# The run length and the pacing of the expert weights that are loaded during the attention

## The chip, the cores and the metric

The kernel runs on one core of a Trainium2 chip. Its engines are TensorE (PE in the profile, with its weight loads as PEld), VectorE (DVE), ScalarE (ACT), GpSimd (POOL) and SyncE (SP, which here only issues transfers). Sixteen DMA engines move the data between HBM and the on-chip memory. The metric is the device time of one execution in microseconds (us), as the median of several runs.

## The reference, cut to what matters

Three layers in a row: attention with a window and global tokens, a soft mixture of 8 experts, and a two-layer network with a squared ReLU. The change touches the weights of the second one, `w1` and `w2` (8 experts, 16 MB each).

```python
# 1. attention: 4 batches x 8 heads, 512 local + 32 global queries, head size 64
out_g = matmul(softmax(q_g @ k_all.T / 8), v_all)
out_l = softmax(window of 32 around each local query, and the 32 global keys) @ v
x = concat([out_g, out_l]) as (2176 tokens, 512)
# 2. soft mixture of experts
logits = x @ phi                                  # (2176, 32): 8 experts x 4 slots
d = softmax(logits, over tokens)
slot_input = (d.T @ x).reshape(8, 4, 512)
for e in range(8):
    h = maximum(slot_input[e] @ w1[e], 0.0)       # w1: (8, 512, 1024)
    slot_out[e] = h @ w2[e]                       # w2: (8, 1024, 512)
x = softmax(logits, over slots) @ slot_out
# 3. relu-squared network
return (maximum(x @ w_in, 0) ** 2) @ w_out        # w_in, w_out held as 64-bit floats
```

## The kernel before, in words

The program has three stages. The **attention** takes the first 156 us. It is cut into 32 steps, four for each of 8 groups (a batch and half of its heads). Each engine executes its instructions in the order in which the program writes them, and that order comes from a list: `at(when, fn)` puts a piece of work at a position `when`, counted in steps, and the list is sorted by `when`. A step `n` has its scores (`emit_S`: matmuls into `s`, line L397, then on VectorE the masked minimum, L404, and on ScalarE the exponentials, L408), its transposes (`emit_T`: `pT`, L416) and its products with the values (`emit_PV`: `X`, L428). The steps of the global queries (`glob_S`, `glob_T`, `glob_PV`: `sg`, `ggT`, `Xg`) and the running token softmax stand between them.

The **expert stage** (about 156 to 190 us) has one block of weights for each of 32 pieces of work: `hidden(q, kc)` uses a block of `w1` (L878, into `hp`), `outputs(q, m)` one of `w2` (L906, into `so`). A block is 1 MB: 128 partitions, two experts, 1024 words of 4 bytes for each. The trace has 8 records of PE for each block. The **last stage** (from 190 us) is the third layer, with matmuls into `ops` that fill PE.

The blocks are loaded ahead by SyncE, in the order of their use. They lie in a ring of 22 buffers: 13 with the tag `w`, which are free from the start, 5 with the tag `k`, in which the attention keeps q, k and v first (so a block can go there only when the attention has read them for the last time), and 4 with the tag `m`, freed at the attention's end. Later blocks take the place of used ones. So 18 blocks (13 + 5) are meant to be loaded while the attention runs.

- Blocks 0 to 12 are loaded by `ring_halves` in two halves, one for each expert of the pair, each half as two transfers of 256 KB. In each transfer a partition receives one run of 2 KB. The list `PACE` says at which positions a half is issued. Where it names an engine (`"dve"`), that engine first writes one element of the half; the transfer has to wait for that write (L172), so it can't start before VectorE has come to that place in its own work.
- Blocks 13 to 17, and later ones, are loaded by `more_weights` in one transfer of 1 MB, in runs of 4 KB (L157), once `RELEASE` at a position has raised the limit: three blocks at 25.85, one at 27.75, one at 29.15, two at 30.85. They have no pacing write. SyncE waits at each for the buffer to be free.

All transfers of SyncE share eight semaphores in turn, so each one waits until the one eight places before it has landed. SyncE's queue is in order: whatever stands behind a waiting transfer waits too. The loads of q, k and v go through SyncE and, for most of v, through GpSimd's queue; the last of them is issued before 120 us.

Of the kernel before, what the change touches and what calls it, by code (L numbers as in the profile page):

```python
# [9 lines left out]
F32 = mybir.dt.float32  # L10
# [40 lines left out]
POS = {'load0': -7.545, 'sort0': -5.099, 'sort1': -3.55, 'glob_S': 1.806, 'glob_T': 2.7, 'glob_PV': 3.655, 'w1': -2.548, 'w4': -0.34, 'w7': -0.339, 'w10': -1.245, 'w13': 1.7, 'v0': -1.648, 'v1': 0.25, 'x0': 1.756, 'x1': 2.555, 'x2': 3.8, 'x3': 4.158, 'L': 5.351, 'E': 5.8, 'sl': 6.752, 'qg': 1.158}  # L51
LASTPOS = {('glob_S', 6): 0.55, ('glob_T', 6): 1.75, ('glob_PV', 6): 3.35, ('glob_S', 7): -0.3, ('glob_T', 7): 0.35, ('glob_PV', 7): 1.7, ('v0', 7): 0.05, ('v1', 7): 2.05, ('w1', 1): -0.75, ('v0', 0): -0.75, ('sort0', 1): -5.95}
QGF = 0
RELEASE = ((25.85, 3), (27.75, 1), (29.15, 1), (30.85, 2))
EP = 'dve'
EQ = 'act'
EK = 'act'
# [5 lines left out]
PACE = [(2.9, 1, None), (3.9, 1, None)]  # L63
PACE += [(4 * k + d, 1, w) for k in range(1, 6) for d, w in ((0.9, None), (1.7, "dve"), (2.95, None), (3.9, None))]
PACE += [(24.9, 2, None), (25.45, 2, "dve")]
RECTS = 'A0-1 B0-2 C0-4 A2-6 B3-8 C5-10 A7-12 B9-15 A13-15 C11-15'
RING = 13
MORE = 5
# [8 lines left out]
def kernel(  # L77
# [7 lines left out]
    nc = tc.nc  # L85
    const = ctx.enter_context(tc.tile_pool(name="const", bufs=1))
    ring = ctx.enter_context(tc.tile_pool(name="ring", bufs=RING, side="right"))
# [20 lines left out]
    for kind, q in UNITS:  # L108
        es = slice(2 * q, 2 * q + 2)
        for m in range(4):  # L110
            src = (
                w1[es, m * 128:(m + 1) * 128, :].rearrange("e p f -> p e f") if kind == "w1" else
                w2[es, m * 256:(m + 1) * 256, :].rearrange("e (p t) d -> p e (t d)", t=2)
            )
# [3 lines left out]
        specs.insert(i, (("raw", raw_half), None))  # L118
    wt, raw = {}, {}
    w_in32, w_out32 = w_in.bitcast(I32), w_out.bitcast(I32)  # L120
    st = {"next": 0, "limit": RING}

    def slot(tag, shape, dt, nm):
        return ring.tile(shape, dt, tag=tag, name=nm, bufs={"w": RING, "k": MORE, "m": LAST}[tag])
# [36 lines left out]
    part = {}  # L161

    def ring_halves(n, paced):

        for _ in range(n):
            key, src = specs[st["next"]]
            c = part.get("c", 0)
            if c == 0:
                part["t"] = slot("w", list(src.shape), F32, f"ring{st['next']}")
            t = part["t"]  # L170
            if paced:
                (nc.vector if paced == "dve" else nc.gpsimd).memset(t[0:1, c, 0:1], 0.0)  # L172
            for x in (0, 512):
                nc.sync.dma_start(out=t[:, c, x:x + 512], in_=src[:, c, x:x + 512])
            part["c"] = 1 - c
            if c:
                wt[key] = t
                st["next"] += 1
# [527 lines left out]
    def at(when, fn, *args):  # L706
        order.append((when, len(order), fn, args))
# [44 lines left out]
    for when, n, paced in PACE:  # L752
        at(when, ring_halves, n, paced)
    for when, n in RELEASE:
        at(when, release, n)
# [317 lines left out]
    rects = []  # L1073
    for r in RECTS.split():
        a, e = map(int, r[1:].split("-"))
# [167 lines left out]
    for n in range(len(seq)):  # L1243
        credit = min(credit + RATE, 1.2)
        if pieces and n >= START and min(free) <= n:
            kind, f, a, fs = pieces[0]
            if n >= due[kind, f] or (credit >= 1 and not ntile[max(n - 1, -1)]):
                d = 2
# [4 lines left out]
                d = min(d, late)  # L1253
# [61 lines left out]
```

## Time and profile before

| | us |
|---|---|
| median of 3 runs (lowest to highest) | 421.16 (419.94 to 423.27) |
| the profiled execution | 421.35 |
| its span, from the first to the last instruction | 419.3 |
| PE busy | 387.4 (92%) |
| PEld busy | 284.2 (68%) |
| ACT busy | 291.6 (70%) |
| DVE busy | 290.8 (69%) |
| POOL busy | 68.4 (16%) |

Busy times are those of one execution. PE's records overlap a little and their ends are modelled, so 92% is no measure of how near PE is to its peak; where PE waited, and for what, is read from the chain of waits. The transfers moved 70.30 MB, at 168 GB/s over the span, but not evenly: most of it lies ahead of 200 us.

### The profile page before, as it was taken

To read this page: it belongs to the slowest core of one execution; us is meant where nothing else is said; L and a number is where in the kernel's file an instruction comes from. 1 tells how busy PE (TensorE), PEld (TensorE's weight loads), DVE (VectorE), ACT (ScalarE), POOL (GpSimd) and SP (SyncE) were. 2 spreads that over 40 slices of the span, in tenths; PEclk is the share of its full clock that TensorE was granted. 3 is DMA by queue.
4 is the path that set the end of the run, shared out by engine and by line. 5 is a ranking of instruction groups with operands and counts; after the bars stand their busy time and mean duration, and the time that the engine had idled before them with its cause. 6 is when DMAs were issued, how large, how long until landed. Compare 5 with 4: busy or idle time off the path is not lost.

```text
span 419.3 us, 11740 instructions
## 1 busy us (share of the span) xinstructions
PE 387.4 (92%) x4510; PEld 284.2 (68%) x4510; DVE 290.8 (69%) x903; ACT 291.6 (70%) x692; POOL 68.4 (16%) x169
## 2 busy tenths in 40 slices
PE   7978888977997889999899999999999999999995
PEld 6756656655773763336676878878787887888883
DVE  2878668868876541666999967878779776726623
ACT  3649787777895731137997988879688886876670
POOL 7336535535362010000000000000000000000000
PEclk9999999999999999999999999999999999999999
DMA  7668686898998999999431606033030000004403
GB/s 194 142 164 237 214 248 161 256 231 230 264 278 321 361 383 402 400 395 376 144 111 52 202 0 197 6 101 100 2 100 2 1 1 2 0 0 152 150 2 125
DMA packets 50199, 70.30 MB, mean 168 GB/s; under 512 B 16960, under 2 KB 33344, under 8 KB 50144
## 3 DMA queue, kind: packets, MB, share of 16 engines
q1 hardware_dynamic: 48512, 66.40, 48.4%
q0 software_dynamic: 1632, 3.15, 3.7%
q8 instruction: 36, 0.59, 0.6%
q14 instruction: 19, 0.16, 0.1%
HBM read 65.08 MB, written 4.46 MB: 166 GB/s over the span
## 4 chain that ended last, share of the span: by engine, by line
PE 69%; DMA 9%; ACT 8%; DVE 7%; issue 4%; SPq 2%; DVEq 0%; ACTq 0%
PE ops L1120 13%; PE ops L1121 13%; PE ops L1122 13%; DMA ring<-in_moe_w_dram 4%; PE hps L1085 4%; PE s L397 3%; DMA qk<-in_k_l_dram 3%; PE X L428 3%; PE hp L878 2%; PE pT L416 2%; ACT pbuf L408 2%; PE xTp L509 1%; DMA keys<-in_k_l_dram 1%; ACT x_g L499 1%; PE busy L662 1%
## 5 line engine op out<-in xcount | busy, mean ns | idle before, releaser
L1120 PE MATMUL ops<-hl,gh 128*128 128x512 f32 x266 | 105.8, 398 | 0.6 <-DVE oacc L1134 0.3
L1121 PE MATMUL ops<-hl,gh 128*128 128x512 f32 x266 | 105.7, 397 | 0.0
L1122 PE MATMUL ops<-hl,gl 128*128 128x512 f32 x266 | 104.9, 394 | 0.0
L1109 DVE TENSOR_TENSOR gl<-r,gh 128x384 fp32r<-128x384 f32 x96 | 49.8, 531 | 26.0 <-ACT r L1104 25.8
L1092 ACT ACTIVATE r<-hps 128x384 f32<-128x384 f32 x96 | 45.0, 469 | 22.9 <-PE hps L1085 21.7
L1120 PEld LDWEIGHTS ops<-hl,gh 128*128 128x128 f32 x266 | 49.9, 188 | 13.5 <-DVE oacc L1134 1.3
L1122 PEld LDWEIGHTS ops<-hl,gl 128*128 128x128 f32 x266 | 50.1, 188 | 12.2
L408 ACT ACTIVATE pbuf<-pbuf,nm 128x128 f32<-128x128 f32 x128 | 41.1, 393 | 24.8 <-DVE nm L404 24.5
L1121 PEld LDWEIGHTS ops<-hl,gh 128*128 128x128 f32 x266 | 50.0, 188 | 8.1 <-DVE hl L971 0.3
L1100 ACT ACTIVATE gh<-r 128x384 fp32r<-128x384 f32 x96 | 48.8, 508 | 3.0
L1104 ACT ACTIVATE r<-r 128x384 f32<-128x384 f32 x96 | 48.6, 507 | 3.0
L1085 PE MATMUL hps<-cT,wst 128*128 128x384 f32 x96 | 33.7, 353 | 1.2 <-ACT r L1092 1.2
L404 DVE CUSTOM_DVE_ANT_0 pbuf<-s,tbuf 128x128 f32<-128x128 f32 x128 | 29.6, 286 | 6.8 <-PE s L397 6.1
L1136 DVE SCALAR_TENSOR_TENSOR oacc<-ops,oacc 128x512 f32<-128x512 f32 x38 | 24.7, 686 | 4.1 <-PE ops L1122 4.0
L942 ACT ACTIVATE sgvm<-sgvm,ebias 128x512 int32<-128x512 int32 x32 | 22.8, 714 | 6.4 <-DVE sgvm L936 6.3
L1085 PEld LDWEIGHTS hps<-cT,wst 128*128 128x128 f32 x96 | 18.0, 188 | 8.4 <-issue 2.3
L416 PE MATMUL pT<-ident,pbuf 128*128 128x128 f32 x128 | 21.2, 289 | 2.7 <-ACT tbuf L186 2.7
L280 POOL DMA_DIRECT2D v<-in_v_l_dram x36 | 23.4, 659 | 0.0
L948 DVE SCALAR_TENSOR_TENSOR sgvm<-raw,sgvm 128x512 int32<-128x512 int32 x32 | 21.9, 685 | 1.0 <-ACT sgvm L942 1.0
L945 DVE SCALAR_TENSOR_TENSOR sgvm<-raw,sgvm 128x512 f32<-128x512 uint32 x32 | 21.9, 685 | 0.1
L416 PEld LDWEIGHTS pT<-ident,pbuf 128*128 128x128 f32 x128 | 13.9, 143 | 8.5 <-ACT tbuf L186 3.7
L971 DVE TENSOR_TENSOR hl<-sgvm,hl 128x512 fp32r<-128x512 f32 x16 | 11.0, 690 | 11.4 <-ACT hl L966 11.3
(202 smaller groups left out, 672.9 us busy)
## 6 DMA issues: line engine op xcount, KB each, us to landing
ring<-in_moe_w_dram SPq DMA_DIRECT2D x18, 1024.0 KB, 10.5
ring<-in_moe_w_dram SPq DMA_DIRECT2D x52, 256.0 KB, 5.3
raw<-in_moe_w_in_dram SPq DMA_DIRECT2D x16, 512.0 KB, 4.2
raw<-in_moe_w_out_dram SPq DMA_DIRECT2D x16, 512.0 KB, 5.0
out_dram<-oacc SPq DMA_DIRECT2D x16, 256.0 KB, 2.1
qk<-in_q_l_dram SPq DMA_DIRECT2D x15, 256.0 KB, 3.7
qk<-in_k_l_dram SPq DMA_DIRECT2D x15, 256.0 KB, 4.1
v<-in_v_l_dram POOLq DMA_DIRECT2D x30, 96.0 KB, 5.4
```

The source lines that it names most:

```text
L404: nc.vector.tensor_tensor_reduce(out=dst, in0=ps[h % 2][:, h // 2, :], in1=mask[:, uu, :], scale=1.0, scalar=FAR, op0=ALU.add, op1=ALU.min ...
L408: nc.scalar.activation(out=dst, in_=dst, func=AF.Exp, bias=nm[:, h:h + 1], scale=-1.0)
L416: nc.tensor.transpose(ps[:, 128 * h:128 * h + 128], pt[:, h, :], ident)
L1085: nc.tensor.matmul(ps, wst[:, f, :], cT[:, t0:t0 + n], start=True, stop=True)
L1092: nc.scalar.activation(out=r, in_=ps, func=AF.Relu)
L1100: nc.scalar.activation(out=gh, in_=r, func=AF.Square)
L1104: nc.scalar.activation(out=r, in_=r, func=AF.Square)
L1109: eng.tensor_tensor(out=gL, in0=sq, in1=gh.bitcast(F32), op=ALU.subtract)
L1120: nc.tensor.matmul(ob[tt], gh[:, s], hi, start=first, stop=False)
L1121: nc.tensor.matmul(ob[tt], gh[:, s], lo, start=False, stop=False)
L1122: nc.tensor.matmul(ob[tt], gL[:, s], hi, start=False, stop=last)
L1136: nc.vector.scalar_tensor_tensor(out=t, in0=ps, scalar=WS, in1=t, op0=ALU.mult, op1=ALU.add)
```

## The change

Blocks 0 to 12 are still loaded in two halves of two transfers each, but a half is now half of the columns of both experts and no longer the whole of one expert. Each transfer still moves 256 KB, now as two runs of 1 KB in each partition. Blocks 13 to 17 are loaded in the same way, four transfers of 256 KB, in place of one of 1 MB with 4 KB runs. Their halves stand at 25.87, 26.27, and so on to 28.67 (eight halves), and at 29.15 and 29.55, each behind a write of one element by VectorE. `RELEASE` keeps only the two blocks at 30.85. From block 18 on everything is loaded as before.

```diff
-RELEASE = ((25.85, 3), (27.75, 1), (29.15, 1), (30.85, 2))
+RELEASE = ((30.85, 2),)
...
 PACE += [(24.9, 2, None), (25.45, 2, "dve")]
+PACE += [(25.87 + 0.4 * x, 1, "dve") for x in range(8)]
+PACE += [(d, 1, "dve") for d in (29.15, 29.55)]
...
-    st = {"next": 0, "limit": RING}
+    st = {"next": 0, "limit": RING + MORE}
...
             if c == 0:
-                part["t"] = slot("w", list(src.shape), F32, f"ring{st['next']}")
+                tag = "w" if st["next"] < RING else "k"
+                part["t"] = slot(tag, list(src.shape), F32, f"ring{st['next']}")
             t = part["t"]
             if paced:
-                (nc.vector if paced == "dve" else nc.gpsimd).memset(t[0:1, c, 0:1], 0.0)
-            for x in (0, 512):
-                nc.sync.dma_start(out=t[:, c, x:x + 512], in_=src[:, c, x:x + 512])
+                nc.vector.memset(t[0:1, 0, 512 * c:512 * c + 1], 0.0)
+            for x in (512 * c, 512 * c + 256):
+                nc.sync.dma_start(out=t[:, :, x:x + 256], in_=src[:, :, x:x + 256])
             part["c"] = 1 - c
```

On SyncE, before, from the last transfer of block 12 (`ring12`; the number behind a ring is the block's) to the second of the last stage's buffers; the names in brackets are what a transfer waits for, DMAHW being the eight shared semaphores and DMASW those of GpSimd's queue:

```order
L174 DMA ring12_2823<-in_moe_w1_dram 128x512 [waits DMAHW0_49]
L157 DMA ring13_2871<-in_moe_w1_dram 128x2x1024 [waits DMAHW1_49,PE_49,Activation_49]
L157 DMA ring14_2873<-in_moe_w1_dram 128x2x1024 [waits DMAHW2_49,PE_49]
L157 DMA ring15_2875<-in_moe_w1_dram 128x2x1024 [waits DMAHW3_49,PE_49]
L157 DMA ring16_3048<-in_moe_w2_dram 128x2x1024 [waits DMASW3_49,DMASW2_49,DMASW4_49,DMASW1_49,DMASW5_49,DMASW0_49,DMAHW4_49,PE_49,Pool_49]
L157 DMA ring17_3144<-in_moe_w2_dram 128x2x1024 [waits DMAHW5_49,PE_49,Activation_49]
L157 DMA ring18_3257<-in_moe_w2_dram 128x2x1024 [waits DMAHW6_49,PE_49]
```

Five transfers of 1 MB stand there between block 12 and block 18. On SyncE now, from block 16's last transfer to the same place:

```order
L177 DMA ring16_3098<-in_moe_w2_dram 128x2x256 [waits DMAHW0_49]
L177 DMA ring17_3164<-in_moe_w2_dram 128x2x256 [waits DVE_49,DMAHW1_49,PE_49,Activation_49]
L177 DMA ring17_3164<-in_moe_w2_dram 128x2x256 [waits DMAHW2_49]
L177 DMA ring17_3164<-in_moe_w2_dram 128x2x256 [waits DMAHW3_49,DVE_49]
L177 DMA ring17_3164<-in_moe_w2_dram 128x2x256 [waits DMAHW4_49]
L159 DMA ring18_3282<-in_moe_w2_dram 128x2x1024 [waits DMAHW5_49,PE_49]
```

In place of the five there are twenty now, and each waits for the one eight places before it; block 18's follows as before and stands behind block 17's last quarter.

On VectorE now, late in the attention (ISA belongs to `emit_S`, `rcg` to `glob_PV` of group 6, `rc` and `xb` to `emit_PV`, `gm` to `glob_S` of group 7):

```order
L407 ISA nm_2948 128x1
L495 TENSOR_SCALAR rcg_3006<-Xg_2981 128x1
L496 RECIPROCAL rcg_3006<-rcg_3006 128x1
L175 MEMSET ring15_3013 1x1
L438 TENSOR_SCALAR rc_3035<-X_3017 128x4
L439 RECIPROCAL rc_3035<-rc_3035 128x4
L440 TENSOR_TENSOR xb_3034<-X_3017,rc_3035 128x256
L459 TENSOR_REDUCE gm_3053<-sg1_3043 128x1
L460 TENSOR_REDUCE gm_3053<-sg2_3044 128x1
L461 TENSOR_TENSOR gm_3053<-gm_3053 128x1
L175 MEMSET ring15_3013 1x1
```

The two writes for block 15 are new there, one between the steps of `glob_PV` and `emit_PV` and one behind `glob_S`; the rest stands as before. Ten such writes are added in all.

## Rows read from the trace of the kernel before

**Rows 1.** Stretches: length, busy PE, PEld, DVE, ACT, POOL; granted clock; DMA share; GB/s.
```profile
100.00:130.00 30.00, 28.21 (x753) 20.17 (x742) 24.21 (x123) 25.51 (x77) 15.81 (x34) 1.00 1.00 273
130.00:135.00 5.00, 2.41 (x78) 1.07 (x71) 2.98 (x10) 2.99 (x9) 1.83 (x5) 0.99 0.85 317
135.00:140.00 5.00, 4.83 (x95) 3.79 (x95) 2.48 (x13) 2.22 (x7) 0.00 (x0) 0.66 1.03 415
...
175.00:190.00 15.00, 14.32 (x127) 4.80 (x120) 10.16 (x30) 4.63 (x8) 0.30 (x1) 1.00 1.03 396
...
200.00:300.00 100.00, 98.20 (x461) 76.14 (x460) 86.60 (x169) 84.42 (x173) 0.00 (x0) 1.00 0.28 93
```

**Rows 2.** Chain of waits, 100 to 200 us: start, length, what.
```profile
132.76 2.41 issue
...
140.88 0.75 issue
...
171.93 16.66 DMA ring<-in_moe_w_dram
```

**Rows 3.** Timeline of PE, 181 to 190 us, the last block.
```profile
188.64 1.07 PE L906 MATMUL so<-ring,hTz 128*32 128x512 f32 x8 [0.68 <-DMA ring<-in_moe_w_dram]
```

**Rows 4.** DMA queues of 128.4 to 132.6, 132.6 to 133.8, 139.2 to 140.4 us.
```profile
q1 hardware_dynamic: 453, 1.15, 78.3%
...
q8 instruction: 1, 0.02, 5.5%
...
q8 instruction: 1, 0.02, 5.3%
```

**Rows 5.** Chain of waits, 25 to 131 us: start, length, what.
```profile
42.72 1.40 issue
...
58.76 1.08 issue
...
97.67 1.34 issue
...
102.60 1.12 issue
```

**Rows 6.** Packets of 100 to 101, 124 to 126 and 135 to 139 us.
```profile
DMA packets 370, 0.36 MB, mean 363 GB/s; under 512 B 16, under 2 KB 370, under 8 KB 370
...
DMA packets 416, 0.77 MB, mean 384 GB/s; under 512 B 48, under 2 KB 48, under 8 KB 415
...
DMA packets 432, 1.67 MB, mean 417 GB/s; under 512 B 26, under 2 KB 26, under 8 KB 431
```

**Rows 7.** Issues of line 174 (halves) from 99 to 128 us.
```profile
L174 SPq DMA_DIRECT2D ring<-in_moe_w_dram x20: 328/431/1502, 99.2 to 127.3; - x20
```

**Rows 8.** Issues of ring at 127.3, 139.9 and 143.8 us, duration in ns, and their landing.
```profile
L174 SPq DMA_DIRECT2D ring<-in_moe_w_dram x2: 587/946/1304, 125.9 to 127.3; - x2
...
DMA to landing us min/median/max: 3.9/4.2/4.6
...
L157 SPq DMA_DIRECT2D ring<-in_moe_w_dram x1: 367/367/367, 139.9 to 139.9; - x1
...
DMA to landing us min/median/max: 6.4/6.4/6.4
...
L157 SPq DMA_DIRECT2D ring<-in_moe_w_dram x1: 368/368/368, 143.8 to 143.8; - x1
...
DMA to landing us min/median/max: 7.0/7.0/7.0
```

**Rows 9.** The pacing writes of VectorE: ns least, median, most; first and last start.
```profile
L172 DVE MEMSET ring<- x7: 59/59/59, 39.4 to 124.9; 1x1 f32 x7
```

**Rows 10.** Timeline of DVE, 115 to 160 us.
```profile
126.24 0.28 DVE L404 CUSTOM_DVE_ANT_0 pbuf<-s,tbuf 128x128 f32<-128x128 f32 x1
...
130.61 0.16 DVE L493 RECIPROCAL rcg<-rcg 128x1 f32<-128x1 f32 x1
...
140.75 0.08 DVE L404 DVE_READ_ACCUMULATOR2_ANT nm<- 128x1 f32 x1
```

## The prediction

> **What bounds the kernel now.** I read the stretches first, then the chain of waits, then PE's timeline, then the transfers.
>
> The last stage fills PE: 98.2 of the 100 us from 200 to 300 are busy and the DMA engines are at 28% [rows 1]. Nothing of the change runs there, so it can only begin earlier or later. What counts is when the expert stage ends.
>
> The expert stage ends on a transfer. The chain of waits goes back over 16.66 us of a ring transfer that was issued at 171.93 and landed at 188.6 [rows 2]. That is the last block, 31. PE waited 0.68 us for it and began at 188.64 [rows 3]. So two things arrive there almost together: PE, which needs the whole stage from 156 us on, and the stream of transfers, which is full (share 1.03, 396 GB/s from 175 to 190 [rows 1]). Making only one of them earlier gains no more than what the other allows.
>
> PE's side has a hole in the attention. At 132.76 it stood 2.41 us in "issue", a wait that no engine's semaphore explains, and at 140.88 another 0.75 us [rows 2]. In the answer on the DMA queues there is no instruction packet from 128.4 to 132.6, one from 132.6 to 133.8, and one again from 139.2 to 140.4, 0.02 MB each [rows 4]; PE goes on at 132.76 + 2.41 = 135.17 and at 140.88 + 0.75 = 141.63, each time some 1.3 us behind the stretch with the packet. I read both waits as PE waiting for its own instructions, which come through the same DMA engines as the 1 MB blocks. Four more such waits of 1.40, 1.08, 1.34 and 1.12 us stand at 42.72, 58.76, 97.67 and 102.60 [rows 5]. The granted clock from 135 to 140, right behind the long wait, is 0.66 on average [rows 1]: the lower level, 1.2 GHz, for x of 5 us with 0.5x + (5 - x) = 3.3, so x = 3.4 us, which cost PE 1.7 us of work.
>
> The Trainium skill (Runtime: NRT & Kernel Launch, section Instruction fetch mechanics) says that instructions come in blocks of 16 KiB, 256 instructions, by a queue of the engine's own, and that crossing a block's border is mostly hidden. The packet size agrees with the trace, the hiding doesn't: 2.41 us were not hidden. By that rule the waits would be something else and stay, which is the third rival below.
>
> The stream's side has pauses. Block 12's last quarter landed at 127.3 + 3.9 = 131.2, block 17 at 139.9 + 6.4 = 146.3, block 18 at 143.8 + 7.0 = 150.8 [rows 8]. A block is 1.049 MB, so 2.5 us at the 417 GB/s of full 4 KB packets [rows 6]. Five blocks would be 12.6 us and took 15.1: 2.5 us of pauses. Block 18 came 4.5 us behind block 17: 2.0 us of pause, because block 17 and block 18 were issued late (139.9 and 143.8), when their buffers had been freed by a PE that was late itself. From block 18 on the stream has no gap worth counting, so the last block's landing moves with block 18's.
>
> **The change part by part.** All terms are for the landing of the last block, because PE will be there first, as worked out at the end.
>
> *Shorter runs, blocks 0 to 12.* Packets of 1 KB move at 363 GB/s, of 2 KB at 384, both with the engines full [rows 6]. Up to about 99 us the stream has free time and the 6% are hidden by it. From 99 to 128 us there are 20 quarter transfers [rows 7], 5.24 MB, with a DMA share of 1.00 from 100 to 130 [rows 1]: 14.4 us instead of 13.7, **+0.8** (rounded up). Bounds: 0, and +2.1 if all 13.6 MB pay (37.6 instead of 35.5 us).
>
> *Waits for instructions up to 104 us.* They sum to 4.9 us [rows 5]. Shorter packets ahead of the instruction packet can only shorten them. The nearest row is the wait at 102.60: ahead of it, at 100 to 101 us, only 1 KB packets were moving [rows 6], and it was still 1.12 us, against 1.08 to 1.40 for the others. So not much goes: I take **-0.8**, some 0.2 us each. Bounds: 0 and -4.9. What PE gains here the paced loads gain too, since their writes stand in VectorE's work.
>
> *Blocks 13 to 17 in 1 KB runs.* 5.24 MB at 363 GB/s are 14.4 us, 1.8 more than at 417. But the pauses go: twenty quarters queue up eight deep (2 MB, over 5 us of transfer), and the pacing positions come earlier than the data: by the order the first write of block 13 stands ahead of VectorE's work at 126.24, that of block 15 behind that at 130.61 and those of block 17 behind that at 140.75 [rows 10], all less PE's gain, while the stream would get to these blocks at about 131, 137 and 143. So 14.4 in place of 15.1, **-0.7**. Bounds: -2.5 (4 KB speed, no pauses) and +1.8 (1 KB speed, all pauses stay).
>
> The Trainium skill (DMA: Bandwidth & Descriptors, section Rules for kernel authors) asks for 1 MiB or more in a transfer for the highest bandwidth, which speaks against this part. The rows agree in direction, 417 against 363 GB/s, and the 1.8 us above already hold the difference that the trace shows; no run here has short transfers with long runs.
>
> *The pause ahead of block 18.* Its transfer waits for PE's last reading of its buffer (143.8 before). With the two waits gone PE gets there some 4 us earlier, at about 140, while block 17 lands at about 146. So block 18 queues behind block 17 without a gap: **-2.0**. Bounds: 0 and -2.0. Behind it on SyncE stands nothing but later blocks, and no load of the attention.
>
> *The ten writes.* 59 ns each [rows 9], 0.6 us of VectorE. They stand between 126 and 141 us. VectorE waits there for PE most of the time (2.98 and 2.48 us busy of 5 [rows 1]), and no write has an open wait except block 16's, whose buffer GpSimd had read long before. Taken at 0; without that cover 0.6.
>
> *The matmuls* of the 18 blocks wait for halves of columns instead of for one expert each; the blocks are there tens of us before, so 0.
>
> **Sum**: +0.8 - 0.8 - 0.7 - 2.0 = -2.7 us. PE's own gain is 0.8, then 2.0 of the 2.41 (between 1.3, if a wait as at 102.60 is left, and all of it), 0.75, and 1.2 of the clock's 1.7 (VectorE and ScalarE are next in line there): 4.75 us. That is more than 2.7, so the stream sets the end, and PE waits 0.68 + 4.75 - 2.7 = 2.7 us for the last block. The profiled execution took 421.35 us (span 419.3 and 2.1 around it); 421.35 - 2.7 = 418.65, **418.6 us**. The median, 421.16, lies 0.2 below the profiled one, which I leave in the rounding. For scale: this kernel's measurement can tell about 1% from no change.
>
> **The rivals.**
>
> 1. *All waits for instructions go.* For it: the two largest stood behind 4 KB packets, and the packets ahead get shorter everywhere. Against: the 1.12 us at 102.60. The loads' pacing moves by 4.9 instead of 0.8 us: +0.8 - 4.9 - 0.7 - 2.0 = -6.8, 414.5 us.
> 2. *The clock falls at a new place.* PE waits 2.7 us ahead of the last block; a wait of 2.41 us was followed by the lower level for 3.4 us. The same there costs 1.7 us on the transposes and small matmuls behind that block: 420.3 us. Against: most of that work waits for other engines anyway.
> 3. *The waits for instructions stay.* For it: from 128.4 to 132.6 the DMA engines were only 78% in use [rows 4], and the packet was late all the same. Then block 18's buffer comes free at 143.8 as before and it lands at 150.8 as before; the +0.8 falls into the pause. 421.4 us: the change doesn't do anything.
> 4. *Slower: the stream pays and keeps its pauses.* The place is the stream from 99 to 151 us. The pauses may come from how a transfer starts (each waits for the landing of the one eight before) and not from PE's lateness. Then +0.8 for the halves and +1.8 for blocks 13 to 17 stand against nothing: 421.35 + 2.6 = 424.0 us. It decides as soon as less than 2.6 of the 4.5 us of pauses go. For it: four times as many transfers have to start. Against: the quarters up to 131 us came at 384 GB/s under the same rule.
>
> **How the numbers follow.** Forecast 0.40 (its own range 416.5 to 420.5), rival 1 0.17, rival 2 0.15, rival 3 0.16, rival 4 0.12. The range runs from 415.0 (most of rival 1) to 423.5 (most of rival 4, and the writes' 0.6 on rival 3). Faster by over 1% is below 417.0: rival 1 and a quarter of the forecast, 0.27. Slower by over 1% is above 425.4: half of rival 4 and little else, 0.07. Within 1%: 0.66.
>
> **What would show it.** Right: at about 128 to 142 us no PE wait over 0.5 us in "issue", and a granted clock of 1.00 from 135 to 140; block 17 landing at about 146 and block 18 less than 3 us behind it; a first `hp` matmul 4 to 5 us earlier than 156.1; and a PE wait of 2 to 3 us ahead of the last block, which lands at about 186. Wrong: a wait over 2 us in "issue" (rival 3), quarters that land more than 0.75 us apart between 131 and 146 (rival 4), a clock below 1.00 around 187 (rival 2), or a first step of the expert stage more than 6 us earlier (rival 1). The whole would be wrong, too, if the loads of q and k in the attention came late behind the many short pieces, which I took as hidden.

## The result, and the profile after

The changed kernel takes **428.49 us** (median of 20 executions, 423.16 to 435.7), the kernel before 422.12 in the same comparison: a ratio of **1.0126** (95% interval 1.0093 to 1.016), 3.9 to 6.8 us slower. The profiled execution, 430.38 us with a span of 428.6, is one of the disturbed ones, which the ratios here and below leave out and the medians don't, so the two don't agree to the last digit. f2 below is the same kernel once more (profiled execution 429.0 us, span 427.2); where its profile reads differently, that is said.

Stretches of the changed kernel, columns as in [rows 1]:

```profile
25.00:100.00 75.00, 63.92 (x1644) 46.35 (x1645) 54.96 (x272) 54.66 (x162) 35.18 (x72) 0.95 0.85 218
100.00:130.00 30.00, 25.24 (x687) 18.49 (x676) 22.82 (x115) 23.84 (x72) 15.65 (x32) 1.00 0.94 221
130.00:135.00 5.00, 3.78 (x96) 2.10 (x92) 3.10 (x22) 2.16 (x7) 0.81 (x2) 1.00 1.08 345
135.00:140.00 5.00, 3.34 (x128) 1.89 (x126) 3.29 (x16) 3.57 (x11) 1.84 (x5) 1.00 1.09 346
140.00:156.00 16.00, 11.97 (x293) 9.46 (x283) 7.54 (x41) 8.00 (x22) 0.80 (x2) 0.93 1.05 357
156.00:175.00 19.00, 17.81 (x126) 7.78 (x124) 3.42 (x18) 4.68 (x16) 1.32 (x2) 0.79 0.82 307
...
200.00:300.00 100.00, 97.92 (x473) 75.99 (x473) 84.41 (x166) 86.60 (x180) 0.00 (x0) 1.00 0.37 127
```

Two stretches of the kernel before that [rows 1] doesn't have, and three of f2:

```profile
25.00:100.00 75.00, 62.42 (x1692) 44.67 (x1692) 56.93 (x282) 55.51 (x166) 35.64 (x73) 1.00 0.80 220
156.00:175.00 19.00, 18.89 (x165) 6.70 (x169) 6.44 (x33) 2.72 (x4) 0.34 (x1) 1.00 1.03 402
```

```profile
25.00:100.00 75.00, 62.10 (x1582) 45.06 (x1580) 53.75 (x267) 54.06 (x160) 35.16 (x72) 0.95 0.82 211
...
140.00:156.00 16.00, 13.14 (x301) 10.23 (x300) 8.43 (x45) 9.39 (x26) 0.80 (x2) 0.89 0.93 295
156.00:175.00 19.00, 18.30 (x141) 8.43 (x145) 4.39 (x23) 4.04 (x15) 1.31 (x2) 0.91 1.03 409
```

The stretch from 200 to 300 us is as full as in [rows 1]. The loss lies ahead of it. From 100 to 130 us PE was busy 25.24 us instead of 28.21, and the core moved 221 GB/s instead of 273 (26.57 us and 239 GB/s in f2). The clock is whole from 135 to 140, where it was 0.66, but it is down in three other stretches: 75 x 0.05 + 16 x 0.07 + 19 x 0.21 = 8.9 us of PE time lost at the lower level, against 1.7 before. In f2 it is 75 x 0.05 + 16 x 0.11 + 19 x 0.09 = 7.2 us.

The chain of waits from 25 to 170 us (start, length, what), all the waits in "issue" of over 1 us:

```profile
46.55 1.21 issue
...
52.68 2.15 issue
...
81.89 1.46 issue
...
88.08 1.43 issue
...
115.22 1.07 issue
...
126.94 1.11 issue
...
132.71 1.22 issue
...
138.33 1.30 issue
...
143.85 1.39 issue
...
150.71 1.96 issue
```

Five such waits of over 1 us, 7.35 us together [rows 2, 5], have become ten, 14.3 us. The 2.41 us at 132.76 is gone; in its place stand three of 1.2 to 1.4 us, one every 5.6 us. With the shorter ones, "issue" is 12.5% of this chain and 8.9% of the same stretch before: 18.1 and 12.9 us. f2 has only four of over 1 us, 7.31 us together, but 11.6% in all: the larger share comes again, the ten long waits don't.

What these waits are can be read from where they stand. Counted over PE's matmuls and weight loads in order of their start, every wait of over 1 us on the chains of all twenty profiles of this document (86 waits, 25 to 170 us) stands, to within one instruction, behind number 193 plus a multiple of 256: the ten above at 1729, 1985, 3265, 3521, 4801, 5313, 5569, 5825, 6081 and 6337, the 2.41 us of before at 5825. Queue 8, which carries instructions, has 36 packets of 16 KB in each profile, one for every 251 of PE's 9020 matmuls and weight loads. So PE stops where a new block of 256 instructions begins, and the prediction's reading, that it waits there for its own instructions, fits.

PE's timeline, the first step of the expert stage and the last blocks:

```profile
164.24 2.79 PE L881 MATMUL hp<-ring,siT 128*32 128x512 f32 x12 [0.45 <-DVE siT L647]
...
194.01 4.66 PE L909 MATMUL so<-ring,hTz 128*32 128x512 f32 x40
```

The expert stage begins at 164.24 instead of 156.11, 8.1 us late, and from there to the end of the span it takes 264.4 us against 263.2. So in this profile the attention lost nearly all of it, and PE doesn't wait for the last block ([rows 3] had 0.68 us). f2 isn't quite the same:

```profile
161.86 6.88 PE L881 MATMUL hp<-ring,siT 128*32 128x512 f32 x48 [0.45 <-DVE siT L647]
...
196.27 1.06 PE L909 MATMUL so<-ring,hTz 128*32 128x512 f32 x8 [1.03 <-DMA ring<-in_moe_w_dram]
```

There the stage begins 5.8 us late, 2.2 us more are lost behind that point, and PE waits 1.03 us for the last block. The attention has the larger part both times; whether the stream bounds the end differs.

Issues of the last quarter of block 17 and of block 18, with the time to landing:

```profile
L177 SPq DMA_DIRECT2D ring<-in_moe_w_dram x1: 368/368/368, 146.0 to 146.0; - x1
...
DMA to landing us min/median/max: 6.9/6.9/6.9
...
L159 SPq DMA_DIRECT2D ring<-in_moe_w_dram x1: 368/368/368, 147.4 to 147.4; - x1
...
DMA to landing us min/median/max: 8.1/8.1/8.1
```

Block 17 landed at 152.9 (146.3 in [rows 8]) and block 18 at 155.5 (150.8). There is no pause between them any more, and both are late. In f2 they land at 155.2 and 158.7, with some pause left (295 GB/s from 140 to 156 us).

### The profile page after: what moved, and what is told of

The parts are those of the page before. It is cut to its first block, busy times and chain, and to the rows that moved or that the text cites. A ratio compares the mean times of both kernels' runs of the same rounds, so it can differ in the third digit from the quotient of the medians.

```text
span 428.6 us, 11789 instructions
## 1 busy us (share of the span) xinstructions
PE 393.1 (92%) x4510; PEld 287.7 (67%) x4510; DVE 290.1 (68%) x913; ACT 291.8 (68%) x692; POOL 68.6 (16%) x169
## 4 chain that ended last, share of the span: by engine, by line
PE 74%; ACT 8%; DVE 6%; issue 5%; DMA 4%; SPq 2%; POOL 0%; DVEq 0%; ACTq 0%; POOLq 0%
PE ops L1123 13%; PE ops L1124 13%; PE ops L1125 13%; PE hps L1088 4%; PE hp L881 4%; PE so L909 3%; PE s L400 3%; PE pT L419 3%; PE X L431 3%; DMA qk<-in_k_l_dram 2%; ACT pbuf L411 2%; PE xTp L512 1%; ACT x_g L502 1%; PE sl L579 1%; PE wpp L994 1%
## 5 line engine op out<-in xcount | busy, mean ns | idle before, releaser
L1123 PEld LDWEIGHTS ops<-hl,gh 128*128 128x128 f32 x266 | 49.9, 188 | 13.5 <-DVE oacc L1137 1.3
L974 DVE TENSOR_TENSOR hl<-sgvm,hl 128x512 fp32r<-128x512 f32 x16 | 11.0, 690 | 11.4 <-ACT hl L969 11.3
```

Source lines behind the costliest of these rows:

```text
L1123: nc.tensor.matmul(ob[tt], gh[:, s], hi, start=first, stop=False)
```

## The experiments

All ratios are to the kernel before on the same chip; e1 to e4, e5 to e8, e9 to e12, f and g were five groups on four chips, so runs of different groups are compared by their ratios. The last column is the share of "issue" in the chain from 25 to 170 us, of one profiled execution each.

| run | what differs from before | us, median | ratio, 95% interval | issue |
|---|---|---|---|---|
| changed kernel | | 428.49 | 1.0126 (1.0093 to 1.016) | 12.5% |
| e1 | 0 to 12: 1 KB, two experts | 426.58 | 1.0132 (1.0084 to 1.018) | 10.0% |
| e2 | 13 to 17 alone, paced, 1 KB, two experts | 422.55 | 1.0031 (0.9994 to 1.0068) | 7.5% |
| e3 | 13 to 17 paced, 2 KB, one expert | 422.98 | 1.0038 (0.9994 to 1.0082) | 8.7% |
| e4 | 13 to 17 in 1 KB, two experts, not paced | 422.92 | 1.0017 (0.9974 to 1.0059) | 11.3% |
| e5 | 0 to 12: 4 KB, 64 partitions | 438.37 | 1.0412 (1.0355 to 1.0468) | 10.1% |
| e6 | 0 to 12: 512 B, one expert | 424.31 | 1.0037 (0.9997 to 1.0076) | 9.2% |
| e7 | 0 to 12: 1 KB, one expert | 422.86 | 1.0044 (1.0006 to 1.0082) | 7.2% |
| e8 | all 18 paced, 4 KB, 64 partitions | 443.94 | 1.0527 (1.0465 to 1.0588) | 18.7% |
| e9 | 0 to 12: 512 KB transfers, 2 KB, two experts | 430.00 | 1.0148 (1.008 to 1.0215) | 13.5% |
| e10 | 0 to 12: 512 KB transfers, 4 KB, one expert | 427.15 | 1.0088 (1.0046 to 1.0131) | 11.6% |
| e11 | changed kernel, one expert in a half | 424.67 | 1.0024 (0.9981 to 1.0068) | 7.5% |
| e12 | 0 to 12: halves of columns, 2 KB, one expert in a transfer | 424.16 | (6 executions, 416.75 to 426.12) | 8.1% |
| f1 | changed kernel, 2 KB, one expert in a transfer | 424.32 | 1.0042 (1.0006 to 1.0079) | 9.2% |
| f2 | changed kernel again | 428.21 | 1.0106 (1.0053 to 1.0159) | 11.6% |
| f3 | as e11 | 423.00 | 1.0022 (0.999 to 1.0054) | 7.3% |
| f4 | as e12 | 423.95 | 1.0023 (0.9982 to 1.0063) | 8.0% |
| g1 | 13 on: one expert in a transfer | 422.45 | 1.0023 (0.9992 to 1.0053) | 7.1% |
| g2 | 0 to 12: 128 KB transfers, 1 KB, one expert | 432.92 | 1.0249 (1.0194 to 1.0305) | 7.5% |

**Which blocks: e1 to e4.** e1 is the kernel before with this alone:

```diff
-                (nc.vector if paced == "dve" else nc.gpsimd).memset(t[0:1, c, 0:1], 0.0)
-            for x in (0, 512):
-                nc.sync.dma_start(out=t[:, c, x:x + 512], in_=src[:, c, x:x + 512])
+                nc.vector.memset(t[0:1, 0, 512 * c:512 * c + 1], 0.0)
+            for x in (512 * c, 512 * c + 256):
+                nc.sync.dma_start(out=t[:, :, x:x + 256], in_=src[:, :, x:x + 256])
```

e2 is the changed kernel with the old lines for blocks 0 to 12, e3 with the old lines for all 18; e4 is the kernel before with blocks 13 to 17 cut into four transfers of 1 KB runs at their old places, without writes.

> Blocks 0 to 12 in 1 KB runs, blocks 13 to 17 as in the kernel before. Theory A (PE's waits for its own instructions grow wherever the queue of transfers ahead holds many short pieces, and the worst place is the dense stream of blocks 13 to 17): about a third of the loss, ratio to the kernel before 1.002 to 1.006, and the 2.4 us wait near 133 us stays. Theory B (short runs delay the loads of q, k and v all through the attention): most of the loss, 1.008 to 1.013. Rival C (the lower clock, set off by any wait, is the loss): 1.00 to 1.01, with the clock's falls telling which.

> Blocks 13 to 17 paced in 1 KB quarters as in the changed kernel, blocks 0 to 12 in 2 KB runs as before. Theory A: two thirds of the loss, 1.006 to 1.010, waits in issue of 1.1 to 2 us at each block of instructions from 127 to 152 us. Theory B: no loss, 0.995 to 1.002.

> All 18 blocks in halves with 2 KB runs, the last five paced at the changed kernel's places: same transfers of 256 KB and same queue depth, half as many pieces. If the number of pieces ahead sets how late PE's instructions come: waits under 0.6 us from 127 to 152 us, ratio 0.992 to 1.000. If the bytes queued (2 MB) set it: waits as in the changed kernel, ratio 1.004 to 1.010.

> Blocks 13 to 17 in 1 KB quarters, but without the pacing writes, released at the places of the kernel before; blocks 0 to 12 as before. If pieces or bytes in the queue count, the same as with the writes: 1.005 to 1.010. If the ten writes of VectorE cost (held-up VectorE, SyncE behind it), less: 0.998 to 1.003.

The loss is in blocks 0 to 12: e1 loses 1.32%, the changed kernel 1.26%. Pacing blocks 13 to 17 costs or gives nothing that can be measured, with 1 KB or with 2 KB runs, nor do short runs without pacing. So theory A, which had a third of the loss in blocks 0 to 12, is out. In e2 the two steps that should have given 2.7 us can be read by themselves. Chain of waits of e2, 125 to 150 us:

```profile
133.50 1.04 issue
...
138.81 1.70 issue
...
145.98 0.60 issue
```

1.04 + 1.70 + 0.60 = 3.34 us, where before had 2.41 + 0.75 = 3.16 [rows 2]: the long wait was cut up, not removed. And the landings of e2's last quarter of block 17 and of its block 18:

```profile
L182 SPq DMA_DIRECT2D ring<-in_moe_w_dram x1: 368/368/368, 142.3 to 142.3; - x1
...
DMA to landing us min/median/max: 6.0/6.0/6.0
...
L159 SPq DMA_DIRECT2D ring<-in_moe_w_dram x1: 368/368/368, 143.1 to 143.1; - x1
...
DMA to landing us min/median/max: 7.7/7.7/7.7
```

Block 17 comes at 148.3, 2.0 us later than before, and block 18 at 150.8, as before. The pause is filled, with the same bytes in slower packets.

**Which property: run length, e5 to e8.** Theory B1 says that the number of pieces is the cost. Blocks 0 to 12 (in e8 all 18, paced) with other lengths, each half from one expert. e5 and e8 get runs of 4 KB by cutting a half at partition 64, e7 takes 1 KB runs, and e6 in the same way four runs of 512 B to a row:

```diff
-            for x in (0, 512):
-                nc.sync.dma_start(out=t[:, c, x:x + 512], in_=src[:, c, x:x + 512])
+            for p in (0, 64):                                          # e5, e8
+                nc.sync.dma_start(out=t[p:p + 64, c, :], in_=src[p:p + 64, c, :])
+            for x in (0, 256):                                         # e7
+                nc.sync.dma_start(
+                    out=t[:, c, :].rearrange("p (k y) -> p k y", k=2)[:, :, x:x + 256],
+                    in_=src[:, c, :].rearrange("p (k y) -> p k y", k=2)[:, :, x:x + 256],
+                )
```

> Blocks 0 to 12 in 4 KB runs (each transfer of 256 KB takes 64 partitions instead of 128), same size and number of transfers, same places; the rest as in the kernel before. Theory B1 (the number of pieces in the attention's stream is the cost, through everything that waits for the DMA engines): half the pieces of the kernel before, so faster, 0.990 to 0.997. Rival B2 (only short runs of 1 KB and less cost): same, 0.997 to 1.003. Rival A (a long piece holds PE's instruction packet up longer): slower, 1.003 to 1.010, with longer waits in issue.

> Blocks 0 to 12 in runs of 512 bytes, expert halves, same size and number of transfers. Theory B1: four times the pieces of the kernel before, three times the added pieces of e1: 1.025 to 1.045. Rival (the cost is not the pieces but that the halves are columns of both experts): 1.000 to 1.005.

> Blocks 0 to 12 in runs of 1 KB, but with one expert to a half as in the kernel before. Theory B1: like e1, 1.009 to 1.017. Rival (columns of both experts cost): 0.998 to 1.003.

> All 18 blocks paced in halves as in the changed kernel, but in 4 KB runs of 64 partitions. Theory B1: the changed kernel's places without its price, 0.988 to 0.998. If the pacing of the last five gives nothing: as e5.

e7 has e1's packets, as many transfers, the same places, and loses 0.44% instead of 1.32%. Even 512 B runs lose no more by the ratio (though its 12 executions spread from 420.9 to 430.5). So theory B1 fails: the short runs are a small part. e5 and e8, which it had faster than before, were no clean test: over 64 partitions the engines are busier and move less. From 25 to 126 us a 4 KB packet took 279 ns on average in e5, and 193 in e10 below, over 128 partitions. The stretch 25 to 125 us of e5, where before had a share of 0.86 and 231 GB/s:

```profile
25.00:125.00 100.00, 79.64 (x2038) 56.70 (x2028) 69.49 (x336) 67.60 (x198) 44.70 (x93) 0.97 0.92 200
```

In e5 loads of k are 22.1% of the chain, against 7.7% before, and those of v 10.9%, with waits like these:

```profile
79.55 7.20 DMA qk<-in_k_l_dram
...
109.55 9.01 DMA v<-in_v_g_dram
```

**Two experts in a transfer: e9 to e12.** What e1 has and e7 hasn't: each transfer takes its runs from two experts, alternately; w1 and w2 hold an expert in 512 x 1024 floats, so they lie 2 MB apart. The new lines, shortened:

```diff
+            nc.sync.dma_start(out=t[:, :, 512*c:512*c+512], in_=src[:, :, 512*c:512*c+512])   # e9
+            nc.sync.dma_start(out=t[:, c, :], in_=src[:, c, :])                               # e10
+            for e in (0, 1):                                                                  # e12
+                nc.sync.dma_start(out=t[:, e, 512*c:512*c+512], in_=src[:, e, 512*c:512*c+512])
```

e11 is the changed kernel with e7's halves.

> Blocks 0 to 12 in halves of columns of both experts, but one transfer of 512 KB for each half, in runs of 2 KB that alternate between the two experts. Only 13 transfers' halves stand where the changed kernel has two transfers each. Theory M (what costs is that one transfer takes its runs from two experts, 2 MB apart): the loss of e1_first13 comes back, 1.0 to 1.5% above before, 426 to 428 us. Rival R (it is the length of the runs): no loss, within 0.4% of before, 421.5 to 423.5. Rival P (it is the number of transfers): no loss, or up to 0.5% faster, 420 to 422.

> Blocks 0 to 12 in halves of one expert, one transfer of 512 KB with runs of 4 KB on 128 partitions. Theory M: one expert in a transfer, so no loss, 421 to 423 us. A theory by which longer runs hold up the kernel's own small loads and its instruction packets (the slow e5_first13_4k, which also had transfers of 64 partitions): 2 to 4% slower, 430 to 438 us. If only the 64 partitions made that one slow, this one stays within 0.5% of before; packets of 4 KB then take about 167 ns and not 279.

> The changed kernel with one thing undone: each half is one expert, in runs of 1 KB as before that, so no transfer takes its runs from two experts; as many transfers, as many packets, the same writes and places. Theory M: the loss goes, 421.5 to 424 us (e7_first13_1k_exp's 0.4% for the short runs stays). Rival R and rival P (run length, number of transfers): the loss stays, 426 to 430 us.

> Blocks 0 to 12 in halves of columns, each as two transfers of one expert, with runs of 2 KB: as many transfers and packets as before, one expert in each. Theory M: no loss, 421 to 423 us. If what costs is that a half holds columns of both experts (the matmuls and writes then wait for other transfers), or that transfers of the two experts take turns in the queue: 1.0 to 1.5% above before, 426 to 428 us.

e11 (one expert) takes the loss of the changed kernel away though its runs stay at 1 KB, which speaks for the two experts. e9 (two experts) loses 1.48% with runs as long as before's, but it says less: e10, with 512 KB transfers too but one expert, still loses 0.88%, so 0.6% is left for the two experts, and the intervals of the two overlap. e10 was a miss for that theory as the only cause. While blocks 0 to 12 are loaded, its chain has the long kind of "issue":

```profile
54.72 2.69 issue
...
117.13 2.30 issue
```

The Trainium skill (DMA: Bandwidth & Descriptors, section Rules for kernel authors) asks for transfers of 1 MiB or more for the highest bandwidth. In this stage, with small loads and instructions on the same engines, going from 256 KB in 2 KB runs to 512 KB in 4 KB runs lost 0.88% (e10), so the measurement goes against it here. Size and run length changed together in e10, and 1 MB was not tried for blocks 0 to 12.

**The same once more, and controls: f1 to f4.** e12 was unclear and e11's executions spread over 16 us. f1 is the changed kernel with e12's transfers; f2 the changed kernel itself; f3 is e11 again, f4 is e12 again.

> The changed kernel with its halves of columns, its writes and its places, but each of a half's two transfers takes one expert, in runs of 2 KB. Theory M (a transfer that takes its runs from two experts costs): no loss, 421.5 to 424 us. Theory C (the halves of columns, or the writes in them, cost): 427 to 430. Theory S (short runs cost, with or without two experts): also 421.5 to 424, but then f3_after_exp_halves_again has to be slow.

> The changed kernel itself once more, beside the others on the same chip: 426 to 430 us, 1.0 to 1.6% above before. A smaller loss would mean that a part of the difference to e11_after_exp_halves was the chip's.

> The kernel of e11_after_exp_halves (changed kernel, 1 KB runs, one expert in each half) again, because its twelve runs lay between 420 and 436. Theory M: 422 to 425.5, at least 2.5 us below f2_after_again. Theory S: as f2_after_again. If both cost, in between: 425.5 to 427.

> The kernel of e12_first13_cols_2k (blocks 0 to 12 in halves of columns, a transfer for each expert, runs of 2 KB) again, because its six runs lay between 416.8 and 426.1. Theory M: 421 to 424. Theory C: 426 to 428.

f2 against f3 is the cleanest pair: the same number of transfers, packets, writes and places, and only the experts in a transfer differ, with them how a half is cut. 428.21 against 423.00 us. f1 and f4 keep the halves of columns, with one expert in a transfer, and lose 0.42 and 0.23%, so it isn't the columns. f1's interval overlaps f2's; f3's ends about where f2's begins. Chain of waits of f3, 25 to 170 us, all "issue" of over 0.8 us:

```profile
86.78 0.88 issue
...
124.48 0.84 issue
...
138.81 2.59 issue
```

and the same of f2:

```profile
43.12 1.00 issue
...
53.28 2.70 issue
...
102.48 0.82 issue
...
106.89 1.27 issue
...
133.48 1.48 issue
...
139.36 1.86 issue
```

**Everywhere, or only in the attention: g1 and g2.** g1 splits every block from 13 on into one transfer for each expert; g2 cuts blocks 0 to 12 into 128 KB:

```diff
-            nc.sync.dma_start(out=t, in_=src)
+            for e in (0, 1):                                           # g1
+                nc.sync.dma_start(out=t[:, e, :], in_=src[:, e, :])
-            for x in (0, 512):
-                nc.sync.dma_start(out=t[:, c, x:x + 512], in_=src[:, c, x:x + 512])
+            for x in (0, 256, 512, 768):                               # g2
+                nc.sync.dma_start(out=t[:, c, x:x + 256], in_=src[:, c, x:x + 256])
```

> The kernel before, with every block from 13 on (1 MB, runs of 4 KB of both experts) loaded as two transfers of one expert each; blocks 0 to 12 as they are. If a transfer with both experts costs wherever it runs: 0.5 to 1% faster than before, 418 to 420 us, and packets of 4 KB that take less than 160 ns between 176 and 186 us. If it costs only beside the small loads of the attention, as in blocks 0 to 12: within 0.4% of before, 421 to 423.5.

> The kernel before, with blocks 0 to 12 in transfers of 128 KB (1 KB runs, one expert, four for a half) in place of 256 KB. e10_first13_exp_512k lost 0.9% with transfers of 512 KB. If the size of a transfer ahead of the small loads and the instructions is what counts: 0.3 to 0.8% faster than before, 418.5 to 421 us. If the length of the runs is: as e7_first13_1k_exp, 0.2 to 0.5% slower, 422 to 424. If the number of transfers on the queue costs: over 1% slower, 426 or more.

g1 gains nothing: from block 13 on, with runs of 4 KB, two experts in a transfer of 1 MB cost nothing that can be measured against one in 512 KB. The rate says the same of short runs. Packets of 132 to 143 us, where almost only blocks 13 to 17 move, first the changed kernel (two experts), then f3 (one):

```profile
DMA packets 3927, 3.83 MB, mean 348 GB/s; under 512 B 230, under 2 KB 3923, under 8 KB 3923
```

```profile
DMA packets 3878, 3.76 MB, mean 342 GB/s; under 512 B 225, under 2 KB 3876, under 8 KB 3876
```

Beside the small loads, too, the packets themselves are no slower: from 25 to 126 us a 1 KB packet of queue 1, on which the blocks and the loads of q and k come, took 56 ns on average in f2 and in f3, 57 in e1 and 55 in e7.

g2 waits little for instructions (7.5%), yet is the slowest of the 128-partition kernels, by 2.49% against 0.44% for e7, which has the same runs in 256 KB. Eight transfers in flight are 1 MB in g2 and 2 MB in e7, which may be the reason; no run tests it. g2 fails on the other side: its stretches show the stream underfed, at 0.55 and 0.76 from 126 to 144 us,

```profile
126.00:131.00 5.00, 5.00 (x136) 3.21 (x124) 4.15 (x22) 3.01 (x11) 2.40 (x6) 1.00 0.55 169
131.00:144.00 13.00, 11.22 (x337) 7.97 (x335) 9.10 (x47) 9.57 (x29) 2.63 (x7) 1.00 0.76 248
```

and its last block is late, by PE's timeline:

```profile
195.61 1.07 PE L906 MATMUL so<-ring,hTz 128*32 128x512 f32 x8 [2.95 <-DMA ring<-in_moe_w_dram]
```

None of these kernels beats the kernel before.

## Why the prediction was wrong

Forecast 418.6 us, range 415.0 to 423.5; measured 428.49. By its own terms:

- **"Shorter runs, blocks 0 to 12": +0.8, with bounds 0 and +2.1. This is the step that failed.** It was mis-sized: e1 measures +1.32% of 422, 5.6 us (3.5 to 7.6). The run length, which the term priced, was about right: e7 has it alone and loses 1.9 us (0.3 to 3.5). What the term left out is that the new halves take both experts in each transfer. The diff shows it (`t[:, :, x:x + 256]` for `t[:, c, x:x + 512]`), and the prediction saw in it only which matmul waits for what, and priced that at 0. By the ratios, e1 against e7 puts 3.7 us on it, and f2 against f3 3.5.
- **"Waits for instructions up to 104 us": -0.8.** They didn't shrink. All "issue" on the chain from 25 to 104 us is 10.6% before, 11.3% in the changed kernel and 11.7% in f2, or 8.4, 8.9 and 9.2 us; those of over 1 us are 4.94, 6.25 and 2.70 us. From 25 to 170 us they didn't follow the packets' length: e7 (1 KB) and f4 (2 KB) have 7.2 and 8.0%. The share was larger with both experts in a transfer and with larger transfers (e10).
- **"Blocks 13 to 17": -0.7, and "the pause ahead of block 18": -2.0.** Together -2.7; e2 measures +1.3 us (-0.3 to +2.9). In e2 the pause did go, but block 17 came 2.0 us later and block 18 no sooner. The term took 363 GB/s, and the stretch moved 348 in the changed kernel; and it had block 18's buffer free 4 us sooner by PE's gain, which wasn't there.
- **"PE's own gain": 4.75.** Its largest part, 2.0 of the 2.41 us, rested on shorter packets letting the instructions through. e2 has 3.34 us of such waits in that place against 3.16. So, as far as one profile tells, the wait isn't a matter of how long one packet is.
- **The rivals.** Rival 3 (the waits stay, "the change doesn't do anything") is what e2 shows for blocks 13 to 17, 422.55 us beside the 421.4 it gave. Rival 4, slower, gave 424.0, and has another place: a stream that pays for shorter packets and keeps its pauses. In the first profile there are no pauses (share 1.05 to 1.09 from 130 to 156 us); in f2 a part stays (0.93 from 140 to 156). Rival 2 (the clock falls elsewhere) is seen, larger than priced: 8.9 and in f2 7.2 us of PE time lost at the lower level in place of 1.7, not behind the last block but at 25 to 100 and 140 to 175 us. Part of that loss lies where PE wasn't the bound, so it can't be added to the waits. Nor does it tell the slow kernels from the others: e1 has 4.2 us of it and e7, which loses little, 4.9.
- **"The ten writes": 0, and "loads of q and k taken as hidden".** The first held: e2 and e3 have the writes and lose nothing that can be measured. The loads of k were not hidden even before, by the lines below this list, but they didn't become worse: the first profile of the changed kernel has no load of q or k of over 1 us on its chain, f2 has one of 5.98, and f3, which is faster, has 5.94 and 5.29.
- **What would show it.** Of the signs that were named, the clock of 1.00 from 135 to 140 came in both profiles, and the distance of block 18 behind 17 in one (2.6 us; 3.7 in f2); the waits of over 0.5 us, the landing of block 17 and the first `hp` came out against it. PE waits 1.03 us for the last block in f2, which comes at 196 and not at 186, and not at all in the first profile.

The two longest waits for loads of k on the chain of the kernel before:

```profile
75.38 4.46 DMA qk<-in_k_l_dram
...
80.32 6.63 DMA qk<-in_k_l_dram
```

**Shown:** the loss hangs on transfers of blocks 0 to 12 that take their runs from two experts; taking only that away takes most of it away, twice (e11, f3), and e7 against e1 puts it in these blocks. That it needs the attention's loads beside them is suggested by g1, not shown: there the runs and the transfers are longer, too. **Seen along with it, in one profile each:** "issue" at 10.0 to 13.5% of the chain in the four with that property in blocks 0 to 12 (the changed kernel, f2, e1, e9), at 7.1 to 9.2% in the others with transfers of 128 or 256 KB over 128 partitions, and in before, but for e4, 11.3% without a loss. Between kernels that differ in the experts alone, these shares make a difference near that of the spans: 7.3 us and 8.8 for the changed kernel over e11, 6.2 and 6.3 for f2 over f3, 4.1 and 2.8 for e1 over e7. So PE's waits at its blocks of instructions are probably how the time is lost; e10 has 11.6% with one expert, and before has 1.7 points more than e7 without being slower, so they are no measure of it. **Not settled:** why such a transfer delays others. Its own packets are not slower, neither where it runs almost alone (348 against 342 GB/s) nor in the attention (56 against 56 ns), so a price for each packet doesn't explain it. Nor does any run vary the distance: the two runs of a partition lie 2 MB apart in HBM and 4 KB apart in the buffer with two experts, 2 KB apart in both with one, and which of these counts is open. No run here shows the order in which an engine takes up the packets of different queues.

The Trainium skill (Runtime: NRT & Kernel Launch, section Instruction fetch mechanics) has the crossing of a block of instructions mostly hidden. The traces don't agree in this stage: the waits of over 1 us there are 14.3 and 7.31 us in the two profiles of the changed kernel and 7.35 us in that of before.

## What to carry to other kernels

When a diff changes a slice, price everything that the slice changes: how long the runs are, how far apart the places of one transfer lie, how many transfers there are and how large each is. Where a full stream shares the DMA engines with small loads and instructions, test the size of its transfers on both sides before touching anything else (here 128 KB lost 2.5%, against 0.4% for 256 KB with the same runs, and 512 KB 0.9%, with longer runs). And take a second profile before counting waits: one had ten long ones, the next four. A wait that disappears from its place isn't gained until the sum of such waits over the stage has become smaller.

## What the runs showed of the hardware

- PE's waits of over 1 us that no semaphore explains stand a multiple of 256 of its matmuls and weight loads apart, on the same grid of numbers in all twenty profiles (86 waits); the longest took 4.25 us (e9, at 130.59).
- A transfer over 64 partitions with 4 KB runs is slow: e5's engines were busy for 0.92 of 25 to 125 us and moved 200 GB/s, before's 0.86 and 231; its 4 KB packets took 279 ns, and 193 over 128 partitions in e10.
- Two source regions 2 MB apart in one transfer cost 0.8 to 0.9% of this kernel's time in blocks 0 to 12, beside small loads (f2 against f3, e1 against e7), and nothing that could be measured from block 13 on (g1, 1.0023).
- Waits of PE for its instructions weren't shortened by shorter packets: 3.34 us with 1 KB packets in e2, 3.16 with 4 KB before, in the same place.
